# RWKV recurrence with a token-mixing FFN on one core: block transposes by one VectorE step and an exchange through DRAM

## The chip, the cores and the metric

One core of a Trainium2 chip runs the kernel. The metric is the time of one execution on the device in microseconds. TensorE (PE) multiplies matrices and loads their weights (PEld), VectorE (DVE), ScalarE (ACT) and GpSimd (POOL) work on tiles in SBUF and PSUM, and SyncE (SP) issues the DMAs. Every engine works through its own list of instructions in order and waits for others by semaphores.

## The reference

```python
def _attn_ref(r, k, v, w, u):            # B, H, S, D = 4, 8, 768, 48
    state = zeros(B, H, D, D)
    for t in range(S):
        cur = einsum('bhd,bhe->bhde', u[None] * kt, vt)
        y[:, :, t] = einsum('bhd,bhde->bhe', rt, state + cur)
        state = wt[:, :, :, None] * state + einsum('bhd,bhe->bhde', kt, vt)

def _moe_ref(x, U, V, w_ch1, w_ch2):     # x: 4 x 768 x 384 from y
    h = x.transpose(0, 2, 1) @ U @ V     # mixes the tokens, rank 32
    u = x + h.transpose(0, 2, 1)
    return u + maximum(u @ w_ch1, 0) @ w_ch2    # 384 -> 1536 -> 384
```

All is float32.

## The kernel before

**Chunks.** The 4 x 768 tokens are 24 chunks `g` of 128 tokens, six to a batch. A chunk has its heads in pairs: `rk` holds r and k with channels on the partitions. DVE scans w to products F (L390) and Q (L405). `RP` multiplies r by Q (L413) and `KS` multiplies k by F (L418, L420). PE makes the scores (step `AM`, L544, tile `aps`), DVE merges them with the diagonal into A (`CP`, L551), PE makes the inner product `YA` (L622, L632) and the product with the state `YZ` (L645, L649), and ACT copies the result to `xT` (`XE`). For the state of the next chunk PE adds k and v products into `dS` (`DS`, L561), for which k must stand with tokens on the partitions: tile `kn`.

**Turning k and x.** For chunks 0 to 11 PE turns k (`KT`, L522) and ACT copies it to `kn`; for chunks in `TURN_K_DVE` (12 to 23) DVE turns it in 32 x 32 blocks, in four steps of four instructions (`KD`, L679), each writing the block to its final partitions. The same holds for x, which the token mix `GA` (L761) needs with tokens on the partitions (tile `xn`): PE (`XT`, L735) for chunks 0 to 11, DVE (`XD`, L714 and L716) for the others.

**The diagonal.** Chunks 0 to 5 make the products k*r as a step `PR` on DVE or GpSimd and sum them by PE (`MD`, L496); the others load k and r a second time (`LKR`) and use `RK`, `RU` and `RED` (L448, L451, L455). The step `GUARD` (ACT, L429) looks over the w of each chunk.

**FFN.** The tokens are also seven blocks of 384 or 512. Per block: three steps `HP` (token mix to `u`), twelve `UP` (L864), each nine matmuls, and twelve `DN` (L898), again nine each, with three output groups. Weights are kept in a high and a low part, hidden values too (`HH` L869 or L871, `HL` L875). `UADD` is L820, and `O` adds the sum (L916). Before their use the weights are loaded raw and converted (`C2` L302, `C3` L315, an `ADD` on GpSimd, `HI`, `SUB` L339). Late in the program they are loaded again and looked over (`LCK`, `CK`, `CM`).

**The order.** A string `ORDER` gives all steps in sequence, three characters each: two for the step and one for the engine that takes it and for filler matmuls ahead of it. Buffers are given out from pools by this order (`plan`). Each engine gets its own steps in that order, so the string sets every engine's queue, SyncE's too. The lines that put k's and x's turning into steps:

```python
kn = step(
    "KD " + nm, "DVE", lambda i=i: turn_k_blocks(i), [kn], take=[buf["kn"]] if i == 0 else [],
    use=[buf["rk"], buf["kn"]],
)
```

Of the kernel before, what the change touches and what calls it, by code (L numbers as in the profile page):

```python
# [8 lines left out]
F32 = mybir.dt.float32  # L9
# [33 lines left out]
TURN_K_DVE, TURN_X_DVE = [12, 13, 14, 15, 16, 17, 18, 19, 20, 21, 22, 23], [12, 13, 14, 15, 16, 17, 18, 19, 20, 21, 22, 23]  # L43
# [5 lines left out]
def channel_order():  # L49
# [13 lines left out]
    "2x02y02z03003203M03603713803303V03P03R03503N03C03W13413903U00J03Q12-03A13E03X03n03m03w03B10L03o00K03S00M04B0"  # L63
    "3Y03F03b03Z14A03T13a13p02+03x00Q03113r03s01403y10N00003q14D03d03e04K04F00C04b00O03D03v03u13I04a03z14L04E14I1"
    "1600S03G00P03c03t10R03+14P03-03O01700204100T00304J07e04G00U04d04M13H14-04+00104k03J03f04H14f04203h04j04000V0"
    "1504N14O13i03g10504g04e10401B03j05107f11804C04i11900W10704h10E07g14Q04l05214R04m07U00803K04p04n14300F00600l0"
    "4S00907X04500D04o15704415804605305400G07Z00A01C00B17v05004q059G0m00X05500H04c04T01A18204704r00e00n00I17u04V0"
    "0Y01D04W00Z05A05B10o05600a01E05C17V01F07d04s04U11G07x00b00p00s04X00z07h04t00c04u10f04808305D07a04v05E04w0490"
    "0d13k03L00q01H17c04x07b05F05G07i14Y07W08013l00u00g00v04y00+05H00r10h04Z05I00-04z08K05J07j15K05L05M07z01008M0"
    "0t07y11107m05N08U05O01201I07+00i07n05P08N07k07l00j05QC0w07-15R01J05U05S07q07Y15V05W05Y05Z01d05a05T18807o05X1"  # L70
    "5b11P00k01317w07r08L01f08418A07s08V11K01e01W07t08W11L05l08907p11g00x05m05+08101M08P09e01h05-05o01X08X01N05n0"
    "8506005p11i05q08615f00y01r01O15c01Y01R01Z08711S01Q08B06102A05g08w01a09E01T08Q05h08S08C01b05d08n08F08T01j08G0"
    "6205e01U01k02B08m08Y16S06309n05x06T08x15r02305y08Z11c15i08o02C01l01s01V15s01t08R02D01u02E05z05u01m05j01y05t0"
    "1n08O01o08p05v05k08c01v05w08u16408a01w06701p08r01x08b01q02402O08D08d01+08y12506501-08E18H06A01z06802H06B0660"
    "2006W09M08v02F02I02608s08z06X08t02706C02102212j02J08+12808e02G18h02P02K08q18i02V02L09206909h08f09009C06a06U0"
    "2M02c09N12Q09106D06b02N16E02R08g18-12909306G06H02S08j02X09409702W09802q02l06Y09O12T02Y09F02d08k06Z16c06I08l0"
    "9908I09A02U16d12e08J06V12Z02a09H09D02k06J02f02g06K02b16h02m09L02h06M09f09B02n0BH02s09i09I06i12i09o02o06j09K0"
# [24 lines left out]
    "Kg0Kh0Ki0M80Kj0Kk0Kl0M90Km0Kn0Ko0Kp0Ke0Kq0"
# [28 lines left out]
def plan(steps, caps):  # L131
# [24 lines left out]
def rwkv_moe_kernel(ctx, tc, wT, rkT, vN, vS, rkN, uB, uT, uD, U, V, w1, w2, out):  # L156
# [85 lines left out]
    def step(name, eng, fn, after=(), take=(), use=(), alt=None):  # L242

        s = Step(name, eng, fn, after, list(take), list(use), alt)
        steps.append(s)
        return s
# [100 lines left out]
    def chunk(g):  # L347
# [7 lines left out]
        by_pe = g < 6  # L355
# [869 lines left out]
```

## Time and profile before

| | us |
|---|---|
| median of 3 runs | 435.29 |
| fastest, slowest run | 434.91, 436.6 |
| span of the profiled execution | 433.5 |
| PE busy in it | 418.0 (96%) |
| DVE busy | 351.0 (81%) |
| ACT busy | 185.5 (43%) |
| POOL busy | 134.3 (31%) |
| DMA, bytes moved | 57.29 MB |

The profiled execution is one of its own, and its span runs from the first instruction to the last, so it is not quite a run's time. A busy share is the union of an engine's instructions. Matmuls overlap, with modelled ends, so that the time from one start to the next tells more than a duration.

### The profile page before, as it was taken

The page shows a single profiled execution, that of the slowest core. Times are in us where ns is not written, and L with a number is a line of the kernel's source. Part 1 is how long each engine was busy: PE and PEld are TensorE (multiplying, and loading weights), DVE is VectorE, ACT ScalarE, POOL GpSimd, SP SyncE. Part 2 cuts the span into 40 slices and gives each one's busy share as a digit, 9 for nine tenths or more (in the row PEclk, how much of TensorE's full clock was granted, in tenths as well). Part 3 has the DMA queues.
Part 4 walks back from the last instruction along what each step waited for, and adds up shares of the span by engine and source line. Part 5 has one row for each costly group of instructions (what it writes and reads, how often), then busy time and mean ns, then how long its engine had stood idle before and what let it go on. Part 6 is the DMA issues. An engine that isn't in the chain of part 4 may idle for free. (4 is left out here: it accounts for less than half of the span.)

```text
span 433.5 us, 10486 instructions
## 1 busy us (share of the span) xinstructions
PE 418.0 (96%) x4156; PEld 363.0 (84%) x4156; DVE 351.0 (81%) x802; ACT 185.5 (43%) x527; POOL 134.3 (31%) x178
## 2 busy tenths in 40 slices
PE   7987999999999999999999999999989999999994
PEld 5976789999998998787778788888767899999994
DVE  8999999998999999999999999999974237325510
ACT  5999889766443343643044254040332012103400
POOL 5665455635735494322238101041000000000000
PEclk9989899999999999999999999999999999999999
DMA  8989638355826464003226403233002041136001
GB/s 279 327 267 338 204 132 310 110 198 172 272 80 217 123 242 158 23 26 107 98 64 231 119 23 117 81 119 122 8 30 74 1 162 39 36 104 206 2 2 60
DMA packets 23913, 57.29 MB, mean 132 GB/s; under 512 B 2864, under 2 KB 7856, under 8 KB 23856
## 3 DMA queue, kind: packets, MB, share of 16 engines
q1 hardware_dynamic: 23856, 56.54, 39.3%
q8 instruction: 34, 0.56, 0.5%
q14 instruction: 23, 0.19, 0.1%
HBM read 51.81 MB, written 4.72 MB: 130 GB/s over the span
## 5 line engine op out<-in xcount | busy, mean ns | idle before, releaser
L898 PE MATMUL f<-hid,w2h 128*128 128x384 f32 (+1 forms) x504 | 148.5, 364 | 0.0
L864 PE MATMUL f<-u,w1h 128*128 128x384 f32 (+1 forms) x504 | 147.8, 364 | 0.6 <-DVE xT L820 0.3
L864 PEld LDWEIGHTS f<-u,w1h 128*128 128x128 f32 x504 | 92.9, 188 | 12.9 <-issue 1.4
L898 PEld LDWEIGHTS f<-hid,w2h 128*128 128x128 f32 x504 | 92.9, 188 | 10.2 <-issue 0.7
L864 PE MATMUL f<-u,w1l 128*128 128x384 f32 (+1 forms) x252 | 90.8, 360 | 0.0
L898 PE MATMUL f<-hid,w2l 128*128 128x384 f32 (+1 forms) x252 | 90.7, 360 | 0.0
L869 ACT ACTIVATE hid<-f 128x384 fp32r<-128x384 f32 (+1 forms) x60 | 32.2, 538 | 96.9 <-PE f L864 88.9
L875 DVE SCALAR_TENSOR_TENSOR hid<-f,hid 128x384 fp32r<-128x384 f32 (+1 forms) x84 | 50.0, 608 | 11.2 <-ACT hid L869 10.5
L898 PEld LDWEIGHTS f<-hid,w2l 128*128 128x128 f32 x252 | 47.4, 188 | 4.7
L864 PEld LDWEIGHTS f<-u,w1l 128*128 128x128 f32 x252 | 47.4, 188 | 4.0
L679 DVE STREAM_TRANSPOSE kn<-rk 32x128 f32<-32x128 f32 x160 | 48.3, 302 | 2.5
L469 ACT ACTIVATE A<-ident,dv 128x128 f32<-128x128 f32 x140 | 43.8, 391 | 6.0 <-DVE dv L455 4.0
L916 DVE TENSOR_TENSOR xT<-f,xT 128x384 f32<-128x384 f32 (+1 forms) x21 | 12.7, 610 | 38.0 <-PE f L898 37.9
L831 POOL TENSOR_TENSOR u<-xT,u 128x512 fp32r<-128x512 f32 (+1 forms) x10 | 12.3, 1238 | 91.5 <-PE f L864 35.8
L322 POOL TENSOR_TENSOR cva_w<-cva_w,raw_w 128x384 int32<-128x384 int32 x24 | 25.0, 1055 | 41.1 <-DVE cva_w L315 15.7
L405 DVE TENSOR_TENSOR_SCAN Q<-w,starts,qd 128x258 f32<-128x258 f32 x48 | 33.3, 735 | 0.5 <-POOL rk L413 0.2
L551 DVE COPY_PREDICATED A<-maskf,aps 128x1024 f32<-128x1024 uint32 x24 | 31.6, 1315 | 0.4 <-PE aps L544 0.2
L390 DVE TENSOR_TENSOR_SCAN F<-w,qd 128x259 f32<-128x259 f32 x48 | 30.4, 675 | 0.5 <-DMA w<-in_wT 0.4
L716 DVE STREAM_TRANSPOSE xn<-xT 32x192 f32<-32x192 f32 x80 | 29.5, 369 | 1.1
L413 POOL TENSOR_TENSOR rk<-rk,Q 128x512 f32<-128x512 f32 x18 | 21.5, 1193 | 25.4 <-DVE Q L405 25.4
L871 DVE TENSOR_SCALAR hid<-f 128x384 fp32r<-128x384 f32 (+1 forms) x24 | 14.3, 596 | 17.7 <-PE f L864 14.4
L475 POOL TENSOR_SCALAR_AFFINE_SELECT A<-dv 128x128 f32<-128x128 f32 (+1 forms) x39 | 11.7, 333 | 43.1 <-DVE dv L455 20.0
(126 smaller groups left out, 568.2 us busy)
## 6 DMA issues: line engine op xcount, KB each, us to landing
raw_w<-in_w SPq DMA_DIRECT2D x48, 384.0 KB, 3.8
rk<-in_rkT SPq DMA_DIRECT2D x24, 512.0 KB, 5.4
kr<-in_rkN SPq DMA_DIRECT2D x18, 384.0 KB, 4.1
w<-in_wT SPq DMA_DIRECT2D x24, 260.0 KB, 4.0
v<-in_vS SPq DMA_DIRECT2D x24, 224.0 KB, 4.6
out_dram<-xT SPq DMA_DIRECT2D x12, 192.0 KB, 3.5
out_dram<-xT SPq DMA_DIRECT2D x9, 256.0 KB, 4.7
raw_V<-in_V SPq DMA_DIRECT2D x8, 96.0 KB, 3.8
```

The source lines that it names most:

```text
L322: lambda: nc.gpsimd.tensor_tensor(out=d["to"].bitcast(I32), in0=d["a"].bitcast(I32), in1=d["e"], op=ALU.add),
L390: nc.vector.tensor_tensor_scan(out=back(F), data0=back(st["w"]), data1=back(qd, OVER * h), initial=1.0, op0=ALU.mult, op1=ALU.add)
L405: nc.vector.tensor_tensor_scan(out=st["Q"][:, a:e], data0=st["w"][:, a:e], data1=qd[:, a - OVER * h : e - OVER * h], initial=starts[:, h : ...
L413: ENG[eng].tensor_tensor(out=rk[:, 0], in0=rk[:, 0], in1=Qv, op=ALU.mult)
L469: nc.scalar.activation(to, one, AF.Copy, scale=dv[:, NP * i + j : NP * i + j + 1])
L551: nc.vector.copy_predicated(to, mask2, new)
L679: nc.vector.transpose(to[32 * j : 32 * j + 32, :, 32 * i : 32 * i + 32], src[32 * i : 32 * i + 32, :, 32 * j : 32 * j + 32])
L716: nc.vector.transpose(to[q, :, :, r], src[r, :, :, q])
L864: nc.tensor.matmul(ps, wt[:, f, ct, :], u[ct][:, z], start=(m == 0), stop=(m == 8))
L869: nc.scalar.activation(h[:, 0], d["ps", f], AF.Relu)
L875: nc.vector.scalar_tensor_tensor(out=h[:, 1], in0=d["ps", f], scalar=0.0, in1=h[:, 0].bitcast(F32), op0=ALU.max, op1=ALU.subtract)
L898: nc.tensor.matmul(d["o", ct], wt[:, 4 * ct + part, f - 3 * part, :], hid[f][:, z], start=(part == 0 and m == 0), stop=(part == 3 and m == 8),
```

## The change

Chunks 9 and up have k turned on DVE and chunks 6 and up have x turned there. The turning is now one instruction over all 128 partitions (for a pair of x chunks, two), which transposes every 32 x 32 block where it lies (`KB`, `XB`). A step `KW` or `XW` writes the tile to DRAM, and `KL` or `XL` reads it back in four DMAs, a band of 32 partitions each, so that the bands change places. `kn` and `xn` hold their columns in four groups of 32, and the steps that read or fill them follow that: `DS` and `MD` use four 32-wide matmuls where one was 48 or 128 wide. Chunks 6 to 8 now make the diagonal by `PR` and `MD`. For chunks 0 to 8 the look over w (`GUARD`) uses a second load of w (`LWG`) that stands late in the order. `HI`, `DV` and others can now have another engine by a list, and the string `ORDER` is new as a whole. The read of the flag (`PF`) now stands ahead of the last output's sum.

```diff
-TURN_K_DVE, TURN_X_DVE = [12, 13, 14, 15, 16, 17, 18, 19, 20, 21, 22, 23], [12, 13, 14, 15, 16, 17, 18, 19, 20, 21, 22, 23]
+TURN_K_DVE, TURN_X_DVE = [9, 10, 11, 12, 13, 14, 15, 16, 17, 18, 19, 20, 21, 22, 23], [6, 7, 8, 9, 10, 11, 12, 13, 14, 15, 16, 17, 18, 19, 20, 21, 22, 23]
+DIAG_PE, LATE_GUARD = [0, 1, 2, 3, 4, 5, 6, 7, 8], [0, 1, 2, 3, 4, 5, 6, 7, 8]
...
 ORDER = (
-    "2x02y02z03003203M03603713803303V03P03R03503N03C03W13413903U00J03Q12-03A13E03X03n03m03w03B10L03o00K03S00M04B0"
+    "0000100200302x03003103202y03812z03N03301401501603O00403403501701803Q03S00Q03D03E039C3A03B13C13R13F03o03r03s1"
...
-        by_pe = g < 6
+        by_pe = g in DIAG_PE
...
+        def load_again():
+            st["wg"] = place("big", [P, NP * SEG], f"wg_{g}", bwg)
+            nc.sync.dma_start(st["wg"], wT[b, c])
...
-                    nc.tensor.matmul(tr[:, 0, j : j + NP + 1 : NP], st["kr"][:, j, :], u_diag[:, j, :], start=True, stop=True)
+                    for q in range(4):
+                        t = slice(32 * q, 32 * q + 32)
+                        nc.tensor.matmul(
+                            tr[t, 0, j : j + NP + 1 : NP], st["kr"][:, j, t], u_diag[:, j, :], start=True, stop=True
+                        )
...
-        def turn_k_blocks(i):
-            if i == 0:
-                st["kn"] = place("kn", [P, NP, P], f"kn_{g}", buf["kn"])
-            turn_blocks(st["kn"], st["rk"][:, 1], i)
+        def turn_k_blocks():
+            d = st["kt"] = place("big", [P, 4, NP, 32], f"kt_{g}", btk)
+            nc.vector.transpose(d.rearrange("p b j c -> p j b c"), st["rk"][:, 1].rearrange("p j (b c) -> p j b c", c=32))
+
+        def send_k():
+            st["kd"] = dram.tile([4, 32, 4, NP * 32], F32, name=f"kd_{g}")
+            nc.sync.dma_start(st["kd"].rearrange("q a b x -> (q a) (b x)"), st["kt"].rearrange("p b j c -> p (b j c)"))
+
+        def fetch_k():
+            st["kn"] = place("kn", [P, 4, NP, 32], f"kn_{g}", buf["kn"])
+            for i in range(4):
+                nc.sync.dma_start(
+                    st["kn"][32 * i : 32 * i + 32].rearrange("a q j c -> a q (j c)"),
+                    st["kd"][:, :, i].rearrange("q a x -> a q x"),
+                )
...
-                for i in range(2):
-                    r = slice(64 * i, 64 * i + D)
+                for q in range(4):
+                    i = q // 2
+                    r = slice(32 * q, 32 * q + 32)
                     to = dS[r, j, i * D : i * D + D]
...
-                    nc.tensor.matmul(to, kn[:, j, r], v[:, j, r], start=not z_pe, stop=True)
+                    nc.tensor.matmul(to, kn[:, q, j, :], v[:, j, 64 * i : 64 * i + D], start=not z_pe, stop=True)
...
+                kn = step("KB " + nm, "DVE", turn_k_blocks, [ks], take=[btk], use=[buf["rk"]])
+                kn = step("KW " + nm, "SP", send_k, [kn], use=[btk])
+                kn = step("KL " + nm, "SP", fetch_k, [kn], take=[buf["kn"]])
...
-    step("PF", "SP", fetch, [pd])
+    outs[NB - 1, NCT - 1][-1].after.append(step("PF", "SP", fetch, [pd]))
```

The steps for x (`XB`, `XW`, `XL`) are written as those for k, with pieces of 96 values (384 bytes) in the read back where k has 128 (512 bytes).

The order moves work at three places that the prediction speaks of. Names are tiles with the chunk's number in them; a number at the end is the tile's own.

**DVE between the scan of chunk 4 and its next scan, while the first batch's chunks run, before:**

```order
L390 SCALAR_TENSOR_TENSOR F_4_418<-w_4_342,qd_110 128x259 x2
L503 COPY dv_3_421<-trd_3_349 128x8
L437 RECIPROCAL starts_113<-F_4_418 128x2
L438 RECIPROCAL qd_110<-F_4_418 128x2
L551 COPY_PREDICATED A_2_344<-maskf_105,aps_123 128x1024
L405 SCALAR_TENSOR_TENSOR Q_4_510<-w_4_342,starts_113,qd_110 128x258 x2
```

and now:

```order
L394 SCALAR_TENSOR_TENSOR F_4_414<-w_4_394,qd_110 128x259 x2
L417 TENSOR_TENSOR rk_3_291<-rk_3_291,Q_3_396 128x512
L445 RECIPROCAL starts_113<-F_4_414 128x2
L446 RECIPROCAL qd_110<-F_4_414 128x2
L343 TENSOR_TENSOR w1l_133<-cva_w1_1_277,w1h_132 128x384
L422 TENSOR_TENSOR kr_5_439<-rk_5_437 128x256
L424 TENSOR_TENSOR kr_5_439<-rk_5_437 128x256
L422 TENSOR_TENSOR kr_4_457<-rk_4_455 128x256
L424 TENSOR_TENSOR kr_4_457<-rk_4_455 128x256
L578 COPY_PREDICATED A_1_378<-maskf_105,aps_123 128x1024
L409 SCALAR_TENSOR_TENSOR Q_4_507<-w_4_394,starts_113,qd_110 128x258 x2
```

The products `PR` of chunks 5 and 4 (two instructions each) and the `RP` of chunk 3 now stand on DVE ahead of the second scan of chunk 4, and the merge there is that of chunk 1 and no longer that of chunk 2.

**DVE and SyncE around the turning of k of chunk 21, before (DVE):**

```order
L875 SCALAR_TENSOR_TENSOR hid_3_10_3805<-f1_3_10_3778,hid_3_10_3805 128x512
L679 STREAM_TRANSPOSE kn_21_3818<-rk_21_3601 32x4x32 x4
L820 TENSOR_TENSOR xT_4_2869<-hp_4_1_3832,xT_4_2869 128x512
L455 TENSOR_REDUCE dv_22_3835<-kr_22_3244 128x8
L390 SCALAR_TENSOR_TENSOR F_22_3837<-w_22_3792,qd_110 128x259 x2
L679 STREAM_TRANSPOSE kn_21_3818<-rk_21_3601 32x4x32 x4
```

now on DVE:

```order
L906 TENSOR_SCALAR hid_4_3_4323<-f1_4_3_4313 128x512
L910 SCALAR_TENSOR_TENSOR hid_4_3_4323<-f1_4_3_4313,hid_4_3_4323 128x512
L1119 TENSOR_REDUCE ends_136<-raw_w2_0_4325 128x1
L540 STREAM_TRANSPOSE kt_21_4336<-rk_21_3905 128x4x4x32
L729 STREAM_TRANSPOSE xt_3_1_4342<-xT_5_3879 128x3x4x32 x2
```

and on SyncE:

```order
L544 DMA kd_22_4334<-kt_22_4258 128x512
L544 DMA kd_21_4338<-kt_21_4336 128x512
L371 DMA kr_23_4340<-in_rkN 128x768
L735 DMA xd_3_1_4355<-xt_3_1_4342 128x2x384
L549 DMA kn_21_4357<-kd_21_4338 32x4x128 x4
L954 DMA out_0_dram<-xT_3_2324 128x512
L745 DMA xn_3_0_4526<-xd_3_1_4355 32x8x96 x4
L549 DMA kn_22_4561<-kd_22_4334 32x4x128 x4
```

Sixteen instructions on DVE (eight of them in these rows) have become one, and on SyncE five DMAs per k and per x pair now stand among the loads and the outputs.

**PE at the state add of chunk 21, before:**

```order
L898 MATMUL f2_3_2_4006<-hid_3_11_3603,w2h_134 128x512
L561 MATMUL dS_126<-v_21_3762,kn_21_3818 48x48 x8
L544 MATMUL aps_123<-rk_22_3927 64x128 x4
L544 MATMUL aps_123<-rk_22_3927 64x64 x4
L544 MATMUL aps_123<-rk_22_3927 64x128 x4
```

and now:

```order
L899 MATMUL f1_4_4_4410<-u_4_2_4286,w1h_132 128x512
L571 MATMUL aps_123<-rk_22_4093 64x128 x4
L571 MATMUL aps_123<-rk_22_4093 64x64 x4
L571 MATMUL aps_123<-rk_22_4093 64x128 x4
L571 MATMUL aps_123<-rk_22_4093 64x64 x4
L589 MATMUL dS_126<-v_21_4130,kn_21_4357 32x48 x16
L648 MATMUL y_21_4464<-A_21_4264,v_21_4130 32x128 x8
```

The state add has sixteen matmuls of 32 columns for eight of 48, and it now stands behind the scores of chunk 22.

## Rows read from the trace of the kernel before

**Rows 1.** Stretches (us): busy time and instructions of each engine, PEclk, DMA share, GB/s.

```profile
core 0: us, PE busy (x) PEld busy (x) DVE busy (x) ACT busy (x) POOL busy (x), PEclk, DMA share, GB/s
0.00:59.20 59.20, 52.86 (x898) 42.77 (x898) 56.61 (x123) 50.42 (x153) 34.70 (x47) 0.94 0.83 281
59.20:320.90 261.70, 259.38 (x2700) 221.97 (x2700) 251.88 (x589) 114.56 (x317) 97.54 (x129) 1.00 0.39 127
320.90:428.20 107.30, 105.72 (x567) 98.22 (x567) 42.20 (x92) 20.50 (x58) 2.04 (x2) 1.00 0.20 67
```

**Rows 2.** Timeline of PE at the first FFN matmul: start us, length us, instruction.

```profile
59.16 0.55 PE L735 MATMUL trx<-ident,xT 128*128 128x128 f32 x3
59.46 0.42 PE L864 MATMUL f<-u,w1h 128*128 128x384 f32 x1
```

**Rows 3.** Timeline of PE near the end, matmuls of 384 columns.

```profile
425.00 0.34 PE L898 MATMUL f<-hid,w2h 128*128 128x384 f32 x1
...
425.17 0.34 PE L898 MATMUL f<-hid,w2l 128*128 128x384 f32 x1
```

**Rows 4.** Timeline of PE around the last token mix; idle time before in brackets.

```profile
318.17 0.39 PE L898 MATMUL f<-hid,w2l 128*128 128x512 f32 x1
318.40 0.39 PE L898 MATMUL f<-hid,w2h 128*128 128x512 f32 x1
...
320.85 0.53 PE L761 MATMUL ga<-xn,U_sb 128*32 128x192 f32 x8 [0.68 <-DVE xn L716]
...
325.78 0.91 PE L815 MATMUL hp<-Vst,gs 96*128 96x384 f32 x2 [0.48 <-DVE xT L820]
```

**Rows 5.** Timeline of PE, attention steps of one chunk in the middle.

```profile
191.72 0.90 PE L544 MATMUL aps<-rk 48*64 48x128 f32 x32
192.55 0.56 PE L561 MATMUL dS<-v,kn 128*48 128x48 f32 x16
193.05 0.65 PE L622 MATMUL y<-A,v 128*32 128x128 f32 x16
193.51 0.62 PE L632 MATMUL y<-A,v 128*32 128x128 f32 x16
193.94 0.62 PE L645 MATMUL y<-rk,Z 128*32 128x128 f32 x16
194.38 0.40 PE L649 MATMUL y<-rk,Z 128*32 128x128 f32 x8
194.71 0.50 PE L864 MATMUL f<-u,w1h 128*128 128x512 f32 x1
```

**Rows 6.** Groups of PE instructions by form, 59.2 to 320.9 us: count, busy, mean ns.

```profile
L864 PE MATMUL f<-u,w1h 128*128 128x512 f32 x204 | 66.9, 398 | 0.6 <-DVE xT L820 0.3 <-DVE hid L875 0.3
...
L898 PE MATMUL f<-hid,w2l 128*128 128x384 f32 x72 | 24.2, 336 | 0.0
```

**Rows 7.** Groups of DVE instructions by form, whole span.

```profile
L679 DVE STREAM_TRANSPOSE kn<-rk 32x128 f32<-32x128 f32 x160 | 48.3, 302 | 2.5
...
L716 DVE STREAM_TRANSPOSE xn<-xT 32x192 f32<-32x192 f32 x80 | 29.5, 369 | 1.1
...
L714 DVE STREAM_TRANSPOSE xn<-xT 32x96 f32<-32x96 f32 x32 | 8.6, 269 | 0.4
...
L413 DVE TENSOR_TENSOR rk<-rk,Q 128x512 f32<-128x512 f32 x6 | 4.1, 685 | 0.0
...
L418 DVE TENSOR_TENSOR kr<-rk 128x256 f32<-128x256 f32 x2 | 0.8, 418 | 0.0
```

**Rows 8.** Timeline of DVE in the first 20 us.

```profile
3.70 1.28 DVE L390 TENSOR_TENSOR_SCAN F<-w,qd 128x259 f32<-128x259 f32 x2 [0.40 <-DMA w<-in_wT]
...
19.14 0.41 DVE L420 TENSOR_TENSOR rk<-rk,F 128x256 f32<-128x256 f32 x1
19.48 0.41 DVE L418 TENSOR_TENSOR rk<-rk,F 128x256 f32<-128x256 f32 x1
```

**Rows 9.** DMA: the queue (share of 16 engines), issues (KB, us to landing), issue timeline.

```profile
q1 hardware_dynamic: 23856, 56.54, 39.3%
...
out_dram<-xT SPq DMA_DIRECT2D x9, 256.0 KB, 4.7
...
raw_V<-in_V SPq DMA_DIRECT2D x8, 96.0 KB, 3.8
...
0.81 0.39 SPq L359 DMA_DIRECT2D w<-in_wT  x1
1.26 0.42 SPq L363 DMA_DIRECT2D rk<-in_rkT  x1
```

More of the change, by code (lines that the diff above doesn't have):

```diff
@@ L68 @@
[L68 to L77, printed above, removed]
@@ L242, in step @@
     def step(name, eng, fn, after=(), take=(), use=(), alt=None):
-        s = Step(name, eng, fn, after, list(take), list(use), alt)
+        s = Step(name, eng, fn, after, list(take), list(use), alt.split() if alt else None)
         steps.append(s)
@@ L566, in chunk @@
             if g in TURN_K_DVE:
[L567 to L572 removed]
+                btk = Buf("big")
+                kn = step("KB " + nm, "DVE", turn_k_blocks, [ks], take=[btk], use=[buf["rk"]])
+                kn = step("KW " + nm, "SP", send_k, [kn], use=[btk])
+                kn = step("KL " + nm, "SP", fetch_k, [kn], take=[buf["kn"]])
             else:
@@ L702, in turn, with blocks_of_x, send_x, fetch_x @@
             n = 2 if even and even.get("waits") else 1
-            def blocks_of_x(i):
+            btx = Buf("big")
+            def blocks_of_x():
+                t = d["xt"] = place("big", [P, n, 4, NCT, 32], f"xt_{b}_{c}", btx)
+                for m in range(n):
+                    src = blocks[blk][:, :, (cc + 1 - n + m) * P : (cc + 2 - n + m) * P]
+                    nc.vector.transpose(
+                        t[:, m].rearrange("p b a c -> p a b c"), src.rearrange("p a (b c) -> p a b c", c=32)
+                    )
+            def send_x():
+                d["xd"] = dram.tile([n, 4, 32, 4, NCT * 32], F32, name=f"xd_{b}_{c}")
+                nc.sync.dma_start(
+                    d["xd"].rearrange("m q a b x -> (q a) m (b x)"), d["xt"].rearrange("p m b a c -> p m (b a c)")
+                )
+            def fetch_x():
                 both = hold(c)
@@ L707, in blocks_of_x @@
                     hold(c - 1)
[L708 to L724 removed]
+                to = both[:, c % 2 + 1 - n : c % 2 + 1].rearrange("p m q a c -> p (m q) (a c)")
+                for i in range(4):
+                    nc.sync.dma_start(to[32 * i : 32 * i + 32], d["xd"][:, :, :, i].rearrange("m q a x -> a (m q) x"))
+            xb = step(f"XB{n} {b}.{c}", "DVE", blocks_of_x, after, take=[btx], use=[bx])
+            xw = step(f"XW{n} {b}.{c}", "SP", send_x, [xb], use=[btx])
+            xl = step(
+                f"XL{n} {b}.{c}", "SP", fetch_x, [xw] + ([even["first"]] if even and n == 1 else []),
+                take=[bxn] if n == 2 else take, use=[bxn],
+            )
+            d["first"] = xl
+            last = [xl]
             d["steps"] = last
```

133 lines of the change are left out of this document (64 added, 69 removed).

## Prediction

> **What bounds the kernel now.** I read the stretches first, because averages over the whole span mix three regimes. Until 59.2 us DVE is busy for 56.61 us of 59.20 and PE, though it shows 52.86, works on short attention steps with waits between them [rows 1]; the first FFN matmul starts at 59.46 [rows 2]. From 59.2 to 320.9 both are full: PE 259.38 and DVE 251.88 of 261.70. After 320.9 DVE has 42.20 of 107.30 to do and PE is full alone [rows 1]. So three things set the end: when the first FFN matmul can start, how many PE steps stand behind it, and how much PE loses between them.
>
> A busy PE in these views is not yet a PE at its best pace, since matmuls overlap, so I compare starts. Matmuls of 384 columns follow each other at 0.17 us (425.00, 425.17) [rows 3], those of 512 at 0.23 (318.17, 318.40) [rows 4]. The attention steps take, start to start: scores 0.83 us, the state add DS 0.50, the inner product 0.89, the state product 0.77 [rows 5]. From 59.2 to 320.9 there are 531 matmuls of 512 columns and 432 of 384, in eight groups, of which the first and the last stand in [rows 6]. 531 x 0.23 + 432 x 0.173 = 196.9; 17 inner products 15.1, 16 scores 13.3, 15 state products 11.6, 14 DS 7.0 (counted in the same view); turns, token mix and the rest I put at 10. That is 254 of 261.7: **PE loses about 8 us there**, while it works just behind a DVE that has no slack. A visible piece is the last token mix: GA waits 0.68 us for the last block transposes of x, HP another 0.48 for DVE [rows 4].
>
> **The change, part by part.**
>
> *Transposes on DVE.* Removed are 160 of k (48.3 us), 80 (29.5) and 32 (8.6) of x, 86.4 us together [rows 7]. Their length grows from 269 ns at 96 elements a partition to 369 at 192, 1.04 ns an element. On that line one of 512 takes 0.70 us and one of 384 takes 0.57; twelve k steps (9, 10, 12 to 16, 18 to 22) and eighteen turns of x cost 8.4 + 10.3 = 19 us. If instead a full-height one pays for each of the four bands of 32 partitions, it is 4 x 302 and 4 x 269 ns, 34 us. Either way DVE loses over 50 us, all of it between 59.2 and 320.9. As PE is full there too, this is worth at most the 8 us that PE loses, not 50. Of the 8 I take 5: the waits at step borders go, and I leave 3 for two places where a new wait can arise (below). Bounds 0 and 8.
>
> *The start.* DVE has no slack before the first FFN matmul, so what is put on it there moves that matmul. The new order has five more products k*r (PR) on DVE before it (seven for two: chunks 6 to 8 now make their diagonal on PE, chunks 3 to 5 come over from GpSimd, chunk 1 goes there) and four more RP (six for two). A PR is two instructions of 0.42 us, an RP 0.685 [rows 7]: 5 x 0.84 + 4 x 0.685 = 6.9; one weight conversion more and a SUB, an RU and a RED fewer nearly cancel. In a packed DVE an instruction of 0.41 us starts 0.34 after the one before it, and the turn of U put first fills the 0.40 us in which DVE now waits for the first w [rows 8]: 6.9 x 0.34 / 0.41 - 0.4 = **+5.3**, so 64.8. Low bound +3: more such waits are filled. High bound +8: the loads of U and V now stand ahead of chunk 1 to 3's loads, at 0.45 us of SyncE each for four of them [rows 9], and DVE's longer sum waits for those. The low parts of u that now go to GpSimd, and the check of w that ScalarE no longer makes there, lie beside this.
>
> *PE after the first FFN matmul.* Moved ahead of it or gone: five turns of x (0.30 each, 59.16 to 59.46 [rows 2]), the turns of k of chunks 8, 9 and 10 (about 0.4 each, four such matmuls), and DS 7 (0.50): -3.2. Added: thirteen DS steps of sixteen 32-wide matmuls for eight 48-wide ones. In the rows a DS record x16 takes 0.50 us for pairs of 48 columns, and the inner product moves 128 columns through four 32-wide tiles at 0.46 us per 16 records [rows 5], 29 ns each. The lower bound is 0.50 (four tiles side by side do what two did), the upper 32 x 0.029 = 0.93. I take 0.55, nearest to DS's own row, since its 48 columns are fewer than the 128: +0.7. Upper bound +5.6. Net -2.5. MD with 32-wide tiles lies before the first FFN matmul, where PE has room.
>
> *ACT and GpSimd.* Eight turns fewer to copy, the early checks of w moved to a second load (nine more loads of 260 KB): ACT is busy 114.56 of 261.70 in the middle stretch [rows 1], so neither sets anything. On SyncE the read of the flag now stands ahead of eight stores; DVE's decision that it waits for comes over thirty FFN steps before the end, so the last store is not behind it.
>
> *The exchange.* Every k goes out (256 KB) and comes back in four DMAs, every x pair the same with 384 KB, on SyncE's one queue, and DS or GA waits for it, with YA and all of PE behind them. A store of 256 KB lands 4.7 us after its issue and the smallest frequent load (96 KB) 3.8 [rows 9]; an issue takes 0.45. A round trip is then 0.45 + 4.7 + 4 x 0.45 + 3.8 = 10.7 us. It must be covered by PE work between DVE's turn and its user. Cover by the new order: x of chunk 23 to GA 3.1: two UP and six DN of 9 x 0.23 = 16.6. k 21 to DS 21, the tightest: five UP and one score, 10.35 + 0.83 = 11.2, of which DVE spends some 2.6 before and in the turn, so 8.6. One late wait of 1 to 2 us there is what I have left in the 3.
>
> **The sum.** 64.8 + (428.2 - 59.5 = 368.7) - 2.5 - 5 + the tail from PE's last matmul at 428.2 to the end of the span at 433.5, 5.3 (one add and one store, unchanged) = 431.3. The median of the runs, 435.29, stands 1.7 above this execution's span of 433.5, so I expect **433.0**. About 0.5% (2.2 us) is what a measurement of this kernel can tell from no change, so this lies at the edge of it.
>
> **Rivals.**
> 1. *Nothing is saved behind the start.* PE keeps losing what it loses now, as its 8 us are borders of steps and not DVE. For it: the releasers of PE's idle time name DVE for little over 1 us [rows 4]. Against: DVE has no slack before 320.9 and much after, and PE loses hardly anything there. 433.0 + 5 = 438.0; with half of it 435.5, no change.
> 2. *The start does not move.* DVE's added steps fill waits. 433.0 - 2.3 = 430.7 at the low bound, and some 428 if nothing of it is felt.
> 3. *Slower: the exchange comes too late.* All DMAs pass through SyncE in order; a fetch whose store has not landed holds the loads behind it. By the DMA row, 23,856 packets took 39.3% of sixteen engines' 433.5 us, 114 ns each [rows 9]. A k fetch has 512 packets, an x pair 1,024; if small ones cost as much, that is 3.6 and 7.3 us on sixteen engines, and the k round trip becomes 14.4. DS 21 is then 6 us late, DS 10 and DS 16 (cover about 14 and 15, with other DMAs queued between) 2 to 3 each: 433.0 + 9 = 442. It decides from a k round trip of about 9 us. The Trainium skill, "DMA: Bandwidth & Descriptors", section Specifications, says that line rate needs pieces of at least 512 bytes; x comes back in pieces of 384. No run here shows such a fetch yet.
>
> 4. *The 32-wide DS matmuls go one by one.* Paced like the inner product's records, 29 ns each [rows 5], a DS takes 0.93 us, and thirteen of them cost 4.9 us more than I put in: 437.9, or 436 in between. Against: those records move 128 columns, a DS record 48. The Trainium skill, "TensorEngine Tiling (Array Packing)", section Instruction Overhead, is on this rival's side: it gives every matmul on trn2 some 60 cycles whatever its columns, which at 2.4 GHz is, as an estimate from that page, 25 ns each and 0.8 us a DS, so that the sum would be 436.3. No row here has such a tile, so the trace leaves it open.
>
> **Chances.** The forecast with its better side (rival 2) 0.49; a sum in which start and savings cancel (half of rival 1) 0.22 and rival 4 0.07, together 0.29 near no change; slower 0.22 (the exchange 0.14, a long start without savings 0.08). The range: below, start +3 and all 8 saved, 433.0 - 2.3 - 3 = 427.7, rounded out to 427. Above, start +8 and nothing saved, 433.0 + 2.7 + 5 = 440.7, and most of rival 3: 441.
>
> **What would show it.** Right: the first FFN matmul at 63 to 66 us, DVE's busy time down to about 290 us with all the fall after 60, a stream transpose of 512 elements at 0.7 us, DS at 0.5 to 0.6 us, and matmul starts at 0.17 and 0.23 us right through the middle. Wrong: a first FFN matmul below 61 or above 67; DS near 0.9; PE idle before DS or GA with a DMA of kn or xn as releaser; a middle stretch that still loses 8 us with an idle DVE.

## The result, and the profile of the changed kernel

The changed kernel takes 444.44 us (median of four runs, 439.54 to 447.74), the kernel before 435.10 in the same set. The ratio is 1.012, with an interval of 1.0082 to 1.0159, from fast runs alone, for which two of the four (446.92, the profiled one, and 447.74) are left out as over 1.5% above the fastest. A second set gave 443.15 (440.80 to 444.97) against 435.55, ratio 1.0176 (1.0129 to 1.0224). So it is slower by 1 to 2%, where the forecast had 433.0 and a range up to 441. The rows below are from the profiled execution of the second set, 443.19 with a span of 441.3.

By stretches, with the borders put at the first FFN matmul and at 330 us, which is not the same step as the 320.9 of [rows 1]:

```profile
0.00:72.85 72.85, 53.65 (x1339) 39.10 (x1340) 60.31 (x134) 48.60 (x149) 34.51 (x46) 0.91 0.74 237
72.85:330.00 257.15, 252.91 (x2849) 219.04 (x2848) 201.45 (x373) 116.80 (x336) 87.96 (x111) 1.00 0.66 200
330.00:436.00 106.00, 105.68 (x577) 98.62 (x575) 35.77 (x75) 10.86 (x24) 4.07 (x4) 1.00 0.08 28
```

Against [rows 1], DVE has 50 us less to do in the middle, as forecast, and from the first FFN matmul to the end of PE's last one it is 362.9 us, where it was 368.5 before. The loss is in the start: the first FFN matmul comes at 72.85 us, not at 59.46 [rows 2]. DVE's work ahead of it grew by 3.4 us (56.87 to 60.31), but DVE is idle for 12.5 of those 72.85 us where it was idle for 2.6 before. The granted clock is not the reason: 0.91 here, and 0.82 in a version (e11 below) whose start is 8 us shorter. The start of the kernel before:

```profile
0.00:59.46 59.46, 53.12 (x900) 43.03 (x901) 56.87 (x124) 50.68 (x153) 34.70 (x47) 0.94 0.83 279
```

What PE waited for (releaser, us in total, times, longest):

```profile
PE trk L536 <- POOL rk L422: 3.9, 1, 3.9
PE dS L589 <- issue: 3.8, 2, 2.0
PE dS L589 <- DMA v<-in_vS: 3.6, 1, 3.6
PE trd L508 <- DVE kr L422: 2.2, 1, 2.2
PE f L899 <- DVE hid L910: 1.6, 2, 0.9
PE trd L508 <- issue: 1.4, 1, 1.4
...
PE aps L571 <- POOL rk L417: 0.9, 1, 0.9
...
PE y L671 <- issue: 0.7, 1, 0.7
...
PE trk L536 <- issue: 0.6, 1, 0.6
```

The lines with "issue" are new: PE stood still, and the profile shows nothing that it waited for. There is no such line for PE in the kernel before. The waits of 3.9, 3.6 and 2.2 us, all before 29 us, are new or longer as well, but e3 below has nearly the same ones (3.8, 3.2 and 2.0) and a first FFN matmul 6 us earlier, so they do not carry the loss. The timeline of PE shows four of the stops with "issue", each with the row ahead of it:

```profile
39.99 0.28 PE L675 MATMUL y<-rk,Z 128*32 128x128 f32 x2
41.98 0.23 PE L589 MATMUL dS<-v,kn 128*32 128x48 f32 x1 [1.71 <-issue]
...
44.57 0.33 PE L536 MATMUL trk<-ident,rk 128*128 128x128 f32 x1
45.45 0.55 PE L536 MATMUL trk<-ident,rk 128*128 128x128 f32 x3 [0.56 <-issue]
...
48.31 0.43 PE L508 MATMUL trd<-u_diag,kr 128*32 128x2 f32 x30
50.13 0.20 PE L508 MATMUL trd<-u_diag,kr 128*32 128x2 f32 x2 [1.40 <-issue]
...
55.26 0.20 PE L588 MATMUL dS<-Z,ident 128*32 128x48 f32 x1
57.50 0.20 PE L589 MATMUL dS<-v,kn 128*32 128x48 f32 x1 [2.04 <-issue]
```

Each stop cuts a step in two: a turn after its first matmul, a sum after 30 of 32 records. Data for a step would be waited for at its first instruction. Counted over all of PE's matmul records from 0, they stand at numbers 603, 730, 857 and 984, exactly 127 apart, and the fifth (0.74 us at 138.3) at 2127, nine times 127 later. The first profiled execution stops at the same five numbers, for 1.24, 1.10, 1.13, 2.01 and 2.40 us. The queues (packets, MB, share of 16 engines) show what comes in such portions:

```profile
q1 hardware_dynamic: 45680, 71.13, 52.2%
q8 instruction: 39, 0.64, 0.6%
```

The second row is 39 packets of 16 KB; before, the same queue had 34 with 0.56 MB. PE has 4,760 matmul records and as many weight loads here, 4,156 each before: 244 to a packet in both. 127 matmuls with their 127 weight loads are 254. So the packets hold PE's own instructions, and theory A of the experiments is that PE reaches the end of one before the next has come.

The trace keeps the time of each packet too, and that bears A out. The latest packets of this queue ahead of the five stops' ends landed at 40.70, 44.22, 48.72, 56.04 and 137.83 us; PE's next records start at 41.98, 45.45, 50.13, 57.50 and 139.09, each 1.2 to 1.5 us behind. Over all runs of this case, 32 of the 33 stops of this kind end 1.2 to 1.6 us behind a packet (the other is one of 0.33 us in e10). In the kernel before, by the same count, PE reaches no border less than 1.9 us behind its packet's landing, and it never stopped. A packet takes about 1 us; the five began 1.2 to 5.0 us after PE's first record behind the border before.

How the stops reach DVE stands on ACT and DVE between 58 and 65 us, first ACT, then DVE:

```profile
58.14 1.03 ACT L628 ACTIVATE Z<-dS,tots 128x96 f32<-128x96 f32 x4 [1.91 <-PE dS L589]
...
63.02 0.49 ACT L692 ACTIVATE xT<-y 128x384 f32<-128x384 f32 x1 [1.81 <-PE y L675]
...
63.91 0.52 ACT L336 ACTIVATE w1h<-cva_w 128x384 fp32r<-128x384 f32 x1
```

```profile
59.10 0.35 DVE L306 TENSOR_SCALAR cva_w<-raw_w 128x384 uint32<-128x384 uint32 x1
64.46 0.56 DVE L343 TENSOR_TENSOR w1l<-cva_w,w1h 128x384 fp32r<-128x384 f32 x1 [5.01 <-ACT w1h L336]
```

ACT copies PE's results in order and converts weights in between. Its conversion of w1 stands behind two copies that wait for PE, and DVE's subtraction waits 5.01 us for the conversion, with all its later work behind it. DVE's waits for w1h before the first FFN matmul, first here, then in e3 below:

```profile
DVE w1l L343 <- ACT w1h L336: 6.7, 2, 5.0
```

```profile
DVE w1l L343 <- ACT w1h L336: 2.3, 1, 2.3
```

The other rows that answer to those of before, DVE's turns (groups by form) and the exchange's DMAs (KB, us to landing):

```profile
L729 DVE STREAM_TRANSPOSE xt<-xT 128x384 f32<-128x384 f32 x18 | 9.4, 550 | 3.2 <-ACT xT L692 3.2
L540 DVE STREAM_TRANSPOSE kt<-rk 128x512 f32<-128x512 f32 x12 | 8.4, 703 | 0.6 <-POOL u L866 0.5
```

```profile
kd<-kt SPq DMA_DIRECT2D x12, 256.0 KB, 3.5
...
kn<-kd SPq DMA_DIRECT2D x48, 64.0 KB, 3.2
xn<-xd SPq DMA_DIRECT2D x32, 96.0 KB, 4.6
```

A turn of k takes what the line through [rows 7] gave, 0.70 us, and one of x 0.55 where it gave 0.57. A k round trip is 0.45 + 3.5 + 1.8 + 3.2 = 9.0 us, not 10.7. A state add of 32-wide tiles goes as fast as one of 48-wide ones:

```profile
133.14 0.55 PE L589 MATMUL dS<-v,kn 128*32 128x48 f32 x32
133.62 0.90 PE L571 MATMUL aps<-rk 48*64 48x128 f32 x32
```

That is 0.48 us from start to start, for twice the records.

### The profile page after: what moved, and what is told of

It reads as the page before. It is cut to its first block, busy times and chain, and to the rows that moved or that the text cites. A ratio compares the mean times of both kernels' runs of the same rounds, so it can differ in the third digit from the quotient of the medians.

```text
span 445.1 us, 11624 instructions
## 1 busy us (share of the span) xinstructions
PE 412.5 (93%) x4760; PEld 357.2 (80%) x4760; DVE 298.4 (67%) x580; ACT 176.4 (40%) x508; POOL 126.6 (28%) x160
## 2 busy tenths in 40 slices
DMA packets 45740, 71.94 MB, mean 162 GB/s; under 512 B 13936, under 2 KB 27376, under 8 KB 45680
## 3 DMA queue, kind: packets, MB, share of 16 engines
q1 hardware_dynamic: 45680, 71.13, 51.1%
## 4 chain that ended last, share of the span: by engine, by line
PE 80%; DVE 5%; DMA 4%; issue 3%; POOL 2%; SPq 1%; ACT 1%; DVEq 0%; POOLq 0%; ACTq 0%
PE f L933 33%; PE f L899 29%; PE aps L571 4%; PE y L648 3%; PE y L658 2%; PE y L671 2%; DMA raw_w<-in_w 2%; PE dS L589 1%; DMA raw_V<-in_V 1%; PE hp L850 1%; DVE A L578 1%; SPq L549 1%; PE y L675 1%; DMA kd<-kt 1%; PE ga L796 1%
## 5 line engine op out<-in xcount | busy, mean ns | idle before, releaser
L933 PE MATMUL f<-hid,w2h 128*128 128x384 f32 (+1 forms) x504 | 145.0, 362 | 0.0
L904 ACT ACTIVATE hid<-f 128x384 fp32r<-128x384 f32 (+1 forms) x52 | 27.6, 535 | 103.6 <-PE f L899 100.1
L479 ACT ACTIVATE A<-ident,dv 128x128 f32<-128x128 f32 x152 | 47.6, 392 | 14.3 <-DVE dv L465 10.5
L866 POOL TENSOR_TENSOR u<-xT,u 128x384 fp32r<-128x384 f32 (+1 forms) x12 | 13.1, 1104 | 82.5 <-DVE u L862 51.0
L326 POOL TENSOR_TENSOR cva_w<-cva_w,raw_w 128x384 int32<-128x384 int32 x24 | 26.1, 1098 | 36.4 <-ACT raw_w L313 13.1
L906 DVE TENSOR_SCALAR hid<-f 128x384 fp32r<-128x384 f32 (+1 forms) x32 | 19.4, 607 | 16.7 <-PE f L899 14.4
L417 POOL TENSOR_TENSOR rk<-rk,Q 128x512 f32<-128x512 f32 x14 | 16.9, 1209 | 32.9 <-DVE Q L409 32.8
L571 PE MATMUL aps<-rk 48*64 48x128 f32 (+1 forms) x768 | 22.9, 260 | 2.8 <-POOL rk L417 1.8
L571 PEld LDWEIGHTS aps<-rk 48*64 48x64 f32 x768 | 19.5, 140 | 7.3 <-issue 3.2
L485 POOL TENSOR_SCALAR_AFFINE_SELECT A<-dv 128x128 f32<-128x128 f32 (+1 forms) x30 | 9.6, 355 | 32.4 <-DVE dv L465 17.9
```

The costliest lines, as they stand in the source:

```text
L326: lambda: nc.gpsimd.tensor_tensor(out=d["to"].bitcast(I32), in0=d["a"].bitcast(I32), in1=d["e"], op=ALU.add),
L417: ENG[eng].tensor_tensor(out=rk[:, 0], in0=rk[:, 0], in1=Qv, op=ALU.mult)
L479: nc.scalar.activation(to, one, AF.Copy, scale=dv[:, NP * i + j : NP * i + j + 1])
L571: nc.tensor.matmul(aps[HP * a : HP * a + HP, i, jj, s0:P], rk[r, 1, jj, k0 : k0 + HP], rk[r, 0, jj, s0:P], start=True, stop=True,)
L904: nc.scalar.activation(h[:, 0], d["ps", f], AF.Relu)
L906: nc.vector.tensor_scalar(out=h[:, 0], in0=d["ps", f], scalar1=0.0, scalar2=None, op0=ALU.max)
```

## Experiments

Four theories. **A**: PE waits for the next block of its instructions, since 32-wide tiles make it issue more and shorter ones. **B**: DVE's added steps and the loads set the start. **C**: the exchange holds other loads behind it on SyncE. **D**: the stops belong to the steps that they cut. Between sets the median of the kernel before lies between 435.0 and 435.73 us.

**The changed kernel again** (e1; no edit).

> The changed kernel itself once more, as the base of what follows. Its first trace has PE stopped without any wait at 42.0 (1.24 us), 46.2 (1.10), 50.5 (1.13), 55.4 (2.01) and 136.4 (2.40): 7.9 us, always 127 matmul records or a multiple of 127 apart. Theory A (instruction blocks: PE has to wait for the next 16 KB block of its own instructions, because 32-wide tiles make it issue more and shorter ones): the stops stand at the same records again, at 1 to 2.5 us each, and their sum varies from execution to execution, as the time does (439.5 to 447.7). Theory B (VectorE's added steps and the loads set the start; the stops are accidents of that execution): no stops or at other records, and the first FFN matmul is still late, at 70 us or more. Theory C (the exchange holds the loads behind it on SyncE): GpSimd waits for r and k of chunk 13 to 17 between 180 and 200 us and PE for GpSimd, as in the first trace (1.75 us).

Measured: 443.15 us. Stops at the same records, 6.45 us in all, 5.7 of them ahead of the first FFN matmul. B alone is out, since it gives no reason for such stops; C is there, but with 0.9 us (PE's wait for `rk` at the scores).

**MD with 128-wide tiles** (e2).

```diff
-                    for q in range(4):
-                        t = slice(32 * q, 32 * q + 32)
-                        nc.tensor.matmul(
-                            tr[t, 0, j : j + NP + 1 : NP], st["kr"][:, j, t], u_diag[:, j, :], start=True, stop=True
-                        )
+                    nc.tensor.matmul(tr[:, 0, j : j + NP + 1 : NP], st["kr"][:, j, :], u_diag[:, j, :], start=True, stop=True)
```

> The diagonal's sums (MD) by four 128-wide matmuls as before, not sixteen 32-wide ones; 216 of 4,760 PE records fewer, all in the first 75 us. Theory A: at least half of the stops before the first FFN matmul go (2 to 4 us of 5.5) and that matmul starts 1 to 3 us earlier, since each MD itself takes 0.4 us more: 2 to 3 us faster than the changed kernel in the same set. Theory B: MD is longer by 0.4 us on a PE that waits anyway: the same time within 1 us, or up to 3 us slower. Theory C: no change.

Measured: 440.25 us, 2.9 less than e1; the stops add up to 4.4 us, 2.9 of them in the start, and the first FFN matmul comes at 69.6, 3.2 us earlier. As A expects, with the start 0.2 us beyond its range.

**State adds with 48-wide tiles where PE turns k** (e3), and ACT's copy of k back in the plain layout that they read (not shown).

```diff
+            if g not in TURN_K_DVE:
+                for j in range(NP):
+                    for i in range(2):
+                        r = slice(64 * i, 64 * i + D)
...
+                        nc.tensor.matmul(to, kn[:, j, r], v[:, j, r], start=not z_pe, stop=True)
+                return
             for j in range(NP):
                 for q in range(4):
```

> The state add by 48-wide tiles as before wherever PE turned k (chunks 0 to 8); the exchanged chunks keep 32-wide tiles. 192 PE records fewer, nearly all before 75 us. Theory A: 2 to 4 us of stops go, as many us faster than the changed kernel. Theory B and C: the same time within 1 us.

Measured: 436.72 us (ten runs), ratio to before 1.0042 (1.0017 to 1.0067): 6.4 us less than e1, more than the 2 to 4 expected. One stop is left, at record 856, and the first FFN matmul is at 66.8. Ahead of it the stops are 3.1 us less than in e1 and DVE's idle time is 5.9 us less, 4.4 of that in its wait for w1h. Why DVE gains more than PE lost in stops is not shown in full; ACT's queue between them is the likely place. From the first FFN matmul to the end of PE it is 361.1 us. The start, and the stop that is left:

```profile
0.00:66.83 66.83, 51.52 (x1163) 37.87 (x1164) 60.23 (x134) 48.24 (x149) 35.02 (x46) 0.95 0.79 258
```

```profile
50.16 0.25 PE L586 MATMUL dS<-Z,ident 128*48 128x48 f32 x2
53.00 0.20 PE L587 MATMUL dS<-v,kn 128*48 128x48 f32 x1 [2.59 <-issue]
```

**Both** (e4).

> Both of these: 408 PE records fewer, so that the attention stretch issues about as many as the kernel before. Theory A: no stop without a wait before the first FFN matmul, which starts at 64 to 67 us (the forecast's 64.8, not 71.2), and the time is 4 to 7 us below the changed kernel's: 433 to 437. Theory B: first FFN matmul still at 70 or more, the time within 1.5 us of the changed kernel's. Theory C: stretch from 180 to 200 us unchanged, the time within 1.5 us.

Measured: 439.75 us, no stop over 0.2 us, but the first FFN matmul at 68.0. A was right on the stops and wrong on the time. A 128-wide MD takes 0.81 to 0.91 us where nothing else holds it, a 32-wide 0.36 to 0.38, and nine of them stand in the start; with one stop left to remove, they cost there more than they gave.

```profile
48.93 0.95 PE L506 MATMUL trd<-u_diag,kr 128*128 128x2 f32 x8
49.82 0.90 PE L565 MATMUL aps<-rk 48*64 48x128 f32 x32
```

That is 1.2 of the 3.0 us by which e4 is slower than e3. The rest lies behind the first FFN matmul (363.1 to PE's end, e3 361.1), and no run shows its cause.

**The tiles alone, on the kernel before** (e5): MD (as in the change) and DS with 32-wide tiles, everything else as before. DS:

```diff
-                for i in range(2):
-                    r = slice(64 * i, 64 * i + D)
+                for q in range(4):
+                    i = q // 2
+                    r = slice(32 * q, 32 * q + 32)
...
-                    nc.tensor.matmul(to, kn[:, j, r], v[:, j, r], start=not z_pe, stop=True)
+                    nc.tensor.matmul(to, kn[:, j, r], v[:, j, 64 * i : 64 * i + D], start=not z_pe, stop=True)
```

> The kernel before with nothing changed but the tiles: MD as sixteen 32-wide matmuls and every state add by 32-wide ones, as the changed kernel has them; order, turns and loads of the kernel before. 528 PE records more. Theory A (PE waits for the next 16 KB block of its instructions where it issues short ones fast): PE stops without a wait at borders 127 records apart in the first 60 us, where the kernel before has none, 2 to 6 us in all; the first FFN matmul at 60 to 65 instead of 59.5, the time 436 to 441. Theory B (the late start comes from VectorE's added steps and the loads, not from the tiles): no stops; MD is 0.4 us shorter six times, so the same time or up to 2 us faster.

Measured: 436.67 us, ratio 1.0039 (1.0018 to 1.0059). One stop of 3.74 us, at record 601, in a kernel that had none, and the first FFN matmul at 61.4 instead of 59.5:

```profile
32.77 0.27 PE L650 MATMUL y<-rk,Z 128*32 128x128 f32 x1
36.79 0.86 PE L650 MATMUL y<-rk,Z 128*32 128x128 f32 x11 [3.74 <-issue]
```

The packet ahead of that record landed at 35.57. The tiles bring the stops, and B's "no stops" falls. With this stop of 3.74 us the start comes 1.9 us later; that the shorter MD gave the rest back is likely, not shown.

**The load of chunk 17 ahead of the exchange** (e6): e3 with one step (the load of r and k of chunk 17) moved 22 steps forward in `ORDER`.

> The kernel with 48-wide state adds for chunks 0 to 8 (first FFN matmul at 66.8, one stop of 2.6 us left), and one step of the order moved: the load of r and k of chunk 17 now stands ahead of the fetch of k 15, the stores of k 16 and of an x pair, and a second load of w on SyncE, not behind them. Theory C (the exchange's DMAs on SyncE make this load late): it is issued some 6 us earlier, GpSimd's wait of 4.5 us for it and PE's of 1.8 us at the scores of chunk 17 go, 1.8 to 3 us faster than without the move: 434 to 435. Rival: the load lands earlier but RP of chunk 17 is then late for VectorE's scan or for GpSimd's steps ahead of it, so PE waits at the same place for another releaser and under 1 us is won.

Measured: 437.26 us; e3 had 436.72. Of PE's waits, the first row is e3's, the second e6's:

```profile
PE aps L569 <- POOL rk L417: 1.8, 1, 1.8
```

```profile
PE dS L596 <- DMA kn<-kd: 1.6, 2, 0.9
```

The load lands earlier and the scores no longer wait. Now the fetch of k is late, by 1.6 us in two state adds, and waits for hid grow from 0.6 to 1.7. C is real, but on SyncE one transfer's delay is only handed to the next. The rival was right on the time.

**MD with 64-wide tiles** (e7): e6 with `range(2)` and slices of 64 in MD.

> As the run with the load of chunk 17 moved, and MD by eight 64-wide matmuls instead of sixteen 32-wide ones, 144 PE records fewer. Theory A: the last stop (2.6 us near 50) shrinks below 1 us, while an MD takes 0.05 to 0.2 us more: 1 to 2.5 us faster than with 32-wide MD. If a 64-wide MD costs what the 128-wide did (0.4 us more, nine times), nothing is won, or 1 to 2 us lost.

Measured: 435.41 us, ratio 0.9986 (0.9963 to 1.0009), 1.9 less than e6. One stop of 1.4 us and one of 0.3 are left, where A expected under 1; an MD takes 0.56.

**Work on DVE in lumps** (e8): e3 and, behind each turned tile, four additions into a spare tile.

```diff
             nc.vector.transpose(d.rearrange("p b j c -> p j b c"), st["rk"][:, 1].rearrange("p j (b c) -> p j b c", c=32))
+            for _ in range(4):
+                nc.vector.tensor_tensor(out=spare, in0=st["rk"][:, 1, 0:NCT], in1=st["rk"][:, 1, 1:NP], op=ALU.add)
```

> The kernel with 48-wide state adds for chunks 0 to 8, with work put on VectorE behind every turn in blocks: four additions of 128x384 into a tile that nobody reads, after each of twelve k and eighteen x; 120 of 0.46 us, 55 us, which brings VectorE's busy time back to that of the kernel before, about 353 us. If the forecast's term is right (PE lost some 5 us between the first FFN matmul and the end because VectorE had no slack): 3 to 8 us slower than without them, with PE waiting for VectorE's hid, xT or A in small pieces. Rival: PE's losses were borders of steps; then the same time within 1.5 us.

Measured: 495.54 us, 58.8 more than e3: neither of the two. The additions took 72.6 us (0.59 and 0.62 us each), and one PE wait carries most of it:

```profile
PE f L911 <- DVE hid L922: 34.8, 11, 6.4
```

**The same, spread** (e10): one addition behind each of the 84 `HL`.

> The kernel with 48-wide state adds for chunks 0 to 8, and one addition of 128x384 (0.6 us, read by nobody) on VectorE behind each of the 84 low parts of hidden values: 50 us spread evenly, not in lumps of 2.4 to 5 us behind the turns (which made it 58 us slower). If the 58 us came from the lumps, as the forecast's term has it (a VectorE as full as before loses PE some 5 us): 3 to 12 us slower than without. If the changed order needs VectorE's free time where it stands (every step that PE waits for comes late by what is put ahead of it): 25 us slower or more.

Measured: 456.57 us (five runs, 451.21 to 458.88), ratio 1.0513, 19.9 more than e3, for 54.1 us of additions; PE's waits for hid are 7.7 us in 13 pieces. That lies between the two expectations and settles neither. By the microsecond of work it is some 0.37 us here and 0.81 in e8, so the lumps made about half of e8's cost; but DVE's free time in the new order is not spare either. What these two say of the kernel before is little, because their order is another.

**Borders moved** (e9): the changed kernel with 60 short matmuls at PE's start.

```diff
     warm(8, idle)
+    warm(60, idle[:, 0:64])
```

> The changed kernel with 60 short matmuls (64 columns, nobody reads them) more at PE's start, where PE was idle from 4.9 to 8.8 us; nothing else. Theory A (PE stops at the border of a 16 KB block of its own instructions): the borders move 60 records ahead against the steps, so the stops stand at the same record numbers (603, 730, 857, 984, 2127) but 60 records earlier in the program, in other steps than the state adds of chunks 1 and 4 and the turn and sum they cut before; 3 to 7 us in all, the time 438 to 447. Theory D (a wait that belongs to those steps, for data or for a free accumulator, which the trace doesn't show): the stops stay in the same steps, 60 records later in number.

Measured: 441.85 us. The stops stand at records 603, 858 and 984, as in e1 to within one, but in other steps:

```profile
38.89 0.25 PE L590 MATMUL dS<-v,kn 128*32 128x48 f32 x3
41.19 0.23 PE L590 MATMUL dS<-v,kn 128*32 128x48 f32 x1 [2.05 <-issue]
...
48.37 0.27 PE L590 MATMUL dS<-v,kn 128*32 128x48 f32 x4
49.40 0.53 PE L672 MATMUL y<-rk,Z 128*32 128x128 f32 x12 [0.76 <-issue]
...
53.08 0.27 PE L672 MATMUL y<-rk,Z 128*32 128x128 f32 x1
54.44 0.53 PE L672 MATMUL y<-rk,Z 128*32 128x128 f32 x12 [1.08 <-issue]
```

The first now stands at the end of one state add, where it stood near the start of the next; the second was in a sum of the diagonal, the third in a state add, and both are in state products now. At record 730 there is none this time. They keep their number and change their step, and each ends 1.4 to 1.5 us behind a packet: theory D falls, A stands. From the first FFN matmul (69.9) to PE's end it is 360.8 us.

**Two PR on GpSimd** (e11): e3 with 64-wide MD, and the engine digit of PR 6 and PR 7 changed in `ORDER`.

> 48-wide state adds for chunks 0 to 8, MD by 64-wide matmuls, the order unchanged but for two engines: the products PR of chunks 6 and 7 on GpSimd, which is idle from 40.4 to 43.5, not on VectorE, which is packed from 15 to 56 us. Forecast's term (what VectorE does before the first FFN matmul moves it one for one, 0.67 us a PR): that matmul 1.3 us earlier than in the run with 64-wide MD (67.6 there, with a stop of 1.4): 65 to 66.5, and the time 1 to 2 us below 435.4. Rival (PE's stops and what waits behind them set the start): within 0.5 us of that run.

Measured: 435.05 us, ratio 0.9989 (0.9966 to 1.0012). The first FFN matmul is at 64.87 (65 to 66.5 expected), with no stop over 0.3 us; the time is only 0.4 below e7, so the 1 to 2 us expected of it are not there. The start:

```profile
0.00:64.87 64.87, 53.88 (x1020) 40.28 (x1020) 61.37 (x130) 48.25 (x149) 37.60 (x50) 0.82 0.82 266
```

**Two loads moved as well** (e12): e11 with the load of r and k of chunk 17 moved ahead of the stores of k 16 and of the x pair, and the second load of chunk 0's w behind the fetch of k 16.

> The run with 64-wide MD and two PR on GpSimd (435.05, first FFN matmul at 64.9, no stop over 0.3 us), and two loads moved on SyncE: r and k of chunk 17 ahead of the stores of k 16 and of an x pair, the late second load of w of chunk 0 behind the fetch of k 16. If the waits left are the exchange and that load in each other's way on SyncE (1.2 us at the scores of chunk 17, 1.0 at state adds for k): both go, 433 to 434, faster than both kernels by 0.3% or more. Rival, as when only the load was moved: the wait moves to the next one that is late (VectorE's hid, or the fetch of k 16 all the same) and the time stays within 0.7 us of 435.05.

Measured: 436.32 us, ratio 1.0012 (0.9985 to 1.0039). The scores of chunk 17 wait no more, but stops of 1.5 and 1.0 us are back in a PE program of the same instructions as e11's, and a state add waits 0.9 for k. The rival was right that the waits only move; the time is 1.3 us above e11's, more than its 0.7. No version beats the kernel before by what can be measured; e7 and e11 equal it.

## Why the prediction was wrong

**The start** is where it failed. The text put +5.3 us there (bounds 3 and 8); it was +13.4 in the second profiled execution and +11.8 in the first. The step that failed is the sentence on the tiles, "MD with 32-wide tiles lies before the first FFN matmul, where PE has room". PE has room in time, but with the narrow tiles, and MD for three chunks more, its records for MD and DS ahead of that matmul went from 208 to 640 and all of them from 900 to 1,339. The DS steps ahead of it were put at nothing too. PE then ran out of instructions: 5.7 us of stops in e1, 5.5 in the first execution. With them goes "so neither sets anything" on ACT and GpSimd, which was drawn from the middle stretch alone. ACT's conversions stand in line behind copies of PE's results, so a late PE makes DVE wait (6.7 us). In a start without slack on DVE, that moved everything behind it.

The +5.3 itself priced DVE's added work in a DVE that stays packed. The work grew by 3.4 us, 1.9 less than that; the other 10.0 of the 13.4 us are idle time of DVE, for which the sum had no term. That e11 comes to 64.87, where the sum had 64.8, is in part luck: its DVE is busy for 61.37 us, 1.1 more than in e3 although two PR went to GpSimd, and idle for 3.5. B is thus a part of the truth, and its smaller part.

**PE behind the first FFN matmul and the saved waits**: -2.5 and -5, together -7.5. From the first FFN matmul to PE's end, before had 368.5 us; e9 has 360.8 (-7.7), e3 361.1 (-7.4), e1 362.9 (-5.6). So this sum held in e3 and e9 and was 2 us too good in e1, which has one stop (0.7) and waits for hid (1.6) in it. In e2, e4, e6, e7, e11 and e12 it is 362.1 to 363.8, 1.1 to 2.8 us short of the sum, so e3 and e9 are the best cases and not the rule. The first profiled execution gained nothing there, 368.3: a stop of 2.4 us stands in the middle, with PE's wait for r and k of chunk 17. The 8 us that PE was said to lose were the rest of a sum with an estimate of 10 in it; as idle time the rows have 2.3 (261.70 less 259.38 [rows 1]). How the -7.5 divides into its two terms isn't shown; e8 and e10, meant for that, gave 58.8 and 19.9 us where 3 to 12 were expected.

**The transposes**: 0.70 and 0.55 us, 17.8 us in all where the sum had 19. As foretold, the 50 us that DVE lost in the middle were worth far less: all that PE won there is 0.2 us in the first execution and 4.7 to 7.7 in the others without added work.

**The exchange** (rival 3) was not what made it slower. No state add or token mix waited for it in e1; the round trip is 9.0 us, just at the point from which it was to decide. By the queue's row a packet takes 0.522 x 16 x 441.3 us / 45,680 = 81 ns, not 114, although many are small. Where it hurts is a place that the text only touched on with "holds the loads behind it": r and k of chunk 17 come late, for 0.9 to 1.8 us, and clearing the way for them makes the fetch late (e6).

**Rival 4** was wrong in its mechanism and right by luck that the tiles would cost: DS takes 0.48 us, 0.07 less than put in. The Trainium skill's "TensorEngine Tiling (Array Packing)", section Instruction Overhead, gives every matmul on trn2 an overhead of some 60 cycles. The estimate of 0.8 us laid 32 of them end to end, and that isn't borne out: 32 records in 0.48 us are 15 ns each. What the tiles cost is paid elsewhere, in instructions to be brought in.

**The sum again**, with the measured stretches put in: 433.0 plus the 13.4 - 5.3 = 8.1 us of the start and 1.9 of the middle (7.5 - 5.6) is 443.0; measured 443.15. This says where the miss lies and does not test its cause. Of the 8.1, e3 got 6.0 back by wider state adds alone.

## What to carry to other kernels

Narrower tiles cost nothing in matmul time here (DS 0.48 us for 0.50, MD 0.37 for 0.8 to 0.9), but they are two and four times the instructions. Where a stretch has short instructions only, count them: at the five stops of e1, PE had used up its 127 matmuls in 2.9 to 5.3 us, while in the kernel before, by the same count, the shortest took 5.2. That is no fixed threshold: other portions of 3.0 to 4.5 us passed without a stop (e1, e5, e9). The loss showed as idle time with no releaser, in the middle of a step. An engine that carries a chain's link only now and then (here ACT's weight conversions) passes such stops on to one that has no slack.

## What the runs showed of the hardware

PE stops at borders 127 matmul records apart for 0.2 to 3.7 us, with no wait that the profile names; the stops follow the record number and not the step (e9), and end 1.2 to 1.6 us after a 16 KB packet of the instruction queue has landed. The Trainium skill's "Runtime: NRT & Kernel Launch", section Instruction fetch mechanics, says that instructions come in 16 KiB blocks of 256 and that crossing a border is mostly hidden. The size agrees with the 39 packets in 0.64 MB; that it is hidden holds for the kernel before (no stop) and not for 32-wide tiles. Not every border stops PE, and e11 and e12, with the same PE instructions, have 0 and 2 stops of about 1 us and more. What decides when a packet is begun, the load of the DMA queues for one, was not tried and stays open. It may also account for how the changed kernel's runs spread over 8 us (439.54 to 447.74) where those of the kernel before lie within 2 in the same set (434.82 to 436.6); that is argued, not shown.
